# Two VectorE operations of a weight conversion moved between the row maxima of lone attention

## The chip, the cores and the metric

The kernel runs on one core of a Trainium2 chip. The metric is the device time of one execution in microseconds (us).

## The reference, cut to what matters

Sliding-window attention (2 batches, 8 heads, 768 positions, 64 wide; 8 global keys and the last 96) feeds two expert layers.

```python
scores = scale * np.matmul(q, k.transpose(0, 1, 3, 2)) + bias      # bias: -slope * distance
scores = np.where(keep, scores, -1e9)
a = np.exp(scores - np.max(scores, axis=-1, keepdims=True))
a = a / (np.sum(a, axis=-1, keepdims=True) + 1e-09)
attn = np.matmul(a, v)                                             # (1536, 512) after merging heads
h = attn @ w_in1;  x = (np.maximum(h, 0) + alpha * np.minimum(h, 0)) @ w_out1
h = x @ w_in2;     y = (P(h) / (Q(h) + 1e-6)) @ w_out2             # cubic over quadratic in |h|
```

Inputs and outputs are float32, and the weights arrive as 64-bit numbers (two 32-bit words each).

## The kernel before, in words

Attention is cut into 12 blocks of 128 queries, and each block into two half blocks of four heads. A half block is a *slot* u; its two steps z = 2u and 2u + 1 take two heads each. Slots 0 to 9 are lone attention (`alone`, from the start to about 41 us): nothing but attention runs on TensorE. From slot 10 on the joint slots follow (`joint_slot`): the first expert layer's matmuls on L859 and L930 run between the attention of the later slots. Then the layers run by themselves (`plain_slot`).

Every engine executes its instructions in the order in which the code issues them, so the order of the lines in `alone` is the order on each engine. In slot u this is:

- TensorE: scores of slot u (L518), values of slot u - 3 (L595, L597), transposes of the probabilities of slot u - 2 (L574, L576), transposes of the next keys or queries (L460).
- VectorE: in `biased` the scores plus the mask, with the row maximum of each head as a second result (L537: one instruction for a head, and a short one that reads the accumulator; four heads in a slot, on two banks for each step); the reciprocals of the row sums of slot u - 1 (L562, L563); in even slots from 4 on a copy of eight keys (L473) out of the bank in which TensorE's next transposes land; low halves of the output (L608); in odd slots a copy of transposed probabilities (L582).
- ScalarE: exponentials (L544, which need the row maxima), copies out of PSUM, and the first operation of a conversion (L336).
- GpSimd: four normalisations of the probabilities of slot u - 1 (L556, which need the reciprocals), in slot 3 a copy of keys (L501), in slot 4 the sign constants (L223 to L225), and the high part of a conversion (L343).

Between these stands the *conversion* of the weights: 128 x 512 weights arrive as two words each in `stage`, are put together to float32 and split into a high and a low part. It has six operations: ScalarE scales the upper word (L336, into `de`); VectorE shifts it (L337), adds the sign (L338) and adds the bits of the lower word (L340, into `dx`); GpSimd rounds to the high part (L343); VectorE subtracts that from the whole (L346, the low part `winlo` or `woutlo`), and both parts are queued to be spilled to memory. `begin` puts these as a list into `creeps`, and `creep` issues the next entry. `alone` calls `creep` three times a slot, and an entry that does nothing is a pause. A conversion begins at the end of slots 1, 3, 5, 7 and 9. Before the change L336 stands at the end of the odd slot, L337, L338 and L340 in the even slot, L343 in the next odd slot, and L346 is put into the even slot after that, directly ahead of the next conversion's L337. So the conversion's last VectorE operation ends behind the even slot's reciprocals, and L340 is the last VectorE operation ahead of an odd slot's row maxima. In the first joint slot (s == 0, u = 10) the remaining entries are issued at three places. SyncE issues all large transfers, in order.

Of the kernel before, what the change touches and what calls it, by code (L numbers as in the profile page):

```python
# [14 lines left out]
ALU = mybir.AluOpType  # L15
# [42 lines left out]
def flat(t):  # L58
    return t.rearrange("p c f -> p (c f)")


def words(t):
    return flat(t).bitcast(F32)


class Kernel:
# [249 lines left out]
    def begin(self, start):  # L316
        nc = self.nc
        if not start:
            return
        n = self.started  # L320
        self.started += 1
        m, fc, kind, slot = self.plan[n]
        low, e, y = self.staged(n)[:, :, :, 0], self.de[n % 2].bitcast(I32), self.dx[n % 3]
        hi, lo = (flat(self.slots[slot][kind, part]) for part in PARTS)
        x = words(y)

        def kept():
            if m == 0 and fc < KEPT:
                for part, of in zip(PARTS, (hi, lo)):
                    self.unspilled.append((words(self.spilled[fc][kind, part]), of.bitcast(F32)))  # L330
            self.spill()

        last = self.creeps.pop() if self.creeps else lambda: None
        self.creeps.clear()
        self.creeps += [
            lambda: nc.scalar.mul(self.de[n % 2], self.staged(n)[:, :, :, 1].bitcast(F32), 2.0**-112),  # L336
            lambda: (last(), nc.vector.tensor_scalar(y, e, 3, None, ALU.logical_shift_left)),  # L337
            lambda: nc.vector.scalar_tensor_tensor(y, e, -(2**31), y, ALU.bitwise_and, ALU.bitwise_or),  # L338
            lambda: (
                nc.vector.scalar_tensor_tensor(y, low, 29, y, ALU.logical_shift_right, ALU.bitwise_or),  # L340
                self.load_more() if n >= NST else None,
            ),
            lambda: nc.gpsimd.tensor_scalar(hi, x, 1.0, 1.0, ALU.mult, ALU.mult),  # L343
            lambda: None,
            lambda: None,
            lambda: (nc.vector.tensor_sub(lo, x, hi.bitcast(F32)), kept()),  # L346
        ]
# [67 lines left out]
    def attention_window(self, pool, moe):  # L415
        nc, ident, banks = self.nc, self.ident, self.banks
# [39 lines left out]
        def transpose_in(nm, i, bank, cs=slice(0, NC)):  # L456
            src = self.boot[nm, i] if i < 2 else raw[nm][i % 2]
            t = banks[bank].rearrange("p (c t) -> p c t", c=NC)
            for c in range(cs.start, cs.stop):
                nc.tensor.transpose(t[:, c], src[:, 2 * c : 2 * c + 2].rearrange("p h d -> p (h d)"), ident)  # L460
# [42 lines left out]
        def width(z):  # L503
            return P if (z // 4) % NB == 0 else WIN


        def steps_of(u):
            return (2 * u, 2 * u + 1) if 0 <= u < NU else ()

        def scores(u):  # L510
            for z in steps_of(u):
                i, c = divmod(z, 4)
                qb, w = i % NB, width(z)
                w0 = LEAD + i % KEEP * KST - (w - P)
                passes = ((qall, kall),) if i < WHOLE else ((qhi, khi), (qhi, klo), (qlo, khi))
                for e, (q, k) in enumerate(passes):
                    for j, rows in enumerate(HALF):
                        nc.tensor.matmul(  # L518
                            room(z, j),
                            q[i % 2][rows, c],  # L520
                            k[rows, c, w0 : w0 + w],
                            start=e == 0,
                            stop=e == len(passes) - 1,
                        )

        def room(z, j):
            if z < JOIN:
                return banks[4 * (z % 2) + j][:, : width(z)]
            return banks[j][:, 256 * (z % 2) : 256 * (z % 2) + width(z)]

        def biased(u):
            for z in steps_of(u):
                c, w = z % 4, width(z)
                bm = bm0 if w == P else bm1
                for j in range(2):
                    top = stat[u % 3][:, 2 * (z % 2) + j : 2 * (z % 2) + j + 1]
                    nc.vector.tensor_tensor_reduce(  # L537
                        prob[z % 6][:, j, :w], room(z, j), bm[:, 2 * c + j, :], 1.0, 3.0e38, ALU.add, ALU.min, top
                    )
# [18 lines left out]
        def both_ready(u):  # L558
            if steps_of(u):
                r = rec[u % 2]  # L560
                add = nc.vector.tensor_scalar if u < JOIN // 2 else nc.gpsimd.tensor_scalar
                add(r, stat[u % 3][:, 4:8], 1e-9, 1.0, ALU.add, ALU.mult)  # L562
                nc.vector.reciprocal(r, r)  # L563
                for z in steps_of(u):
                    normalise(z)
# [51 lines left out]
        def inputs(u):  # L617
            some = []
            i, odd = divmod(u + 3, 2)
            if not odd and 2 <= i < NBLK:  # L620
                some.append(("k", i, slice(0, NC)))
            i, odd = divmod(u + 2, 2)
            if not odd and 2 <= i < NBLK:
                some.append(("q", i, slice(0, NC)))
            return some
# [12 lines left out]
        def keys_of_all(u):  # L638
            if u % (2 * NB) == 0 and u < NU:
                global_keys(u)  # L640
            if u in (3, 15):
                lead_keys(u)
# [17 lines left out]
        def low_halves():  # L660
            while lows:
                lows.pop(0)()
# [9 lines left out]
        def alone(u):  # L672
            t = 2 * u - JOIN
            if u:
                scores(u)
            if u == 1:
                transpose_in("q", 1, 2)
                self.turn_alpha()
            if u == 2:
                transpose_in(*inputs(1)[0][:2], 3)  # L680
            biased(u)
            if u == 0:
                split_in("q", 0, 7, far, vector=True)
                split_in("k", 1, 3, vector=True)()
            if u == 1:
                split_in("q", 1, 2, vector=True)
            both_ready(u - 1)
            low_halves()
            keys_of_all(u)
            if u < 2:  # L690
                later_masks(range(4 * u, 4 * u + 4))
            values(u - 3)
            if u in WL:
                self.load_next()
            fetches(u)
            if u == 4:
                self.signs()
            exponentials(2 * u)
            if u == 2:
                split_in(*inputs(1)[0][:2], 3)()  # L700
            low = store_x(u - 3)
            self.creep()
            exponentials(2 * u + 1)
            if u == 1:
                self.alpha_ready()
            low()
            self.creep()
            transpose_p(u - 2, 6)
            copy_p(u - 2, 6, both=u % 2 == 1)
            if u > 1:  # L710
                turn_inputs(u)
            self.begin(t in self.starts or t + 1 in self.starts)
            self.creep()
            self.used += u in (2, 4, 6, 8)
# [37 lines left out]
        for u in range(JOIN // 2):  # L752
            alone(u)
# [91 lines left out]
    def moe(self):  # L845
        nc, steps, banks = self.nc, self.steps, self.banks
# [127 lines left out]
        def joint_slot(s, halves):  # L974
            u = JOIN // 2 + s
            opening, turning = halves or (lambda u: None, lambda u: ())
            if s >= CH + 2 and s < CH + 2 + NEARLY:
                self.reload(s - CH - 2)
            opening(u)
            held = []  # L980
            if s == 0:
                self.creep()
            else:
                while self.creeps:
                    self.creep()
                self.tick(True, 2 * s - 1 in self.starts, spread=True, held=held)
                self.join_step(2)
            first(s)
            halves = leaky(s)
            self.join_step(2)  # L990
            if s == 0:
                self.creep()
            lows = turning(u)
            low = halves()
            for high in held:
                high()
            for more in lows:
                more()
            low()
            if s == 0:  # L1000
                self.creep()
            self.tick(True, 2 * s in self.starts, spread=True)
            if s:
                second(s - 1)
            if s == LATE - 1:
                self.tick(True, 2 * s + 1 in self.starts)
                self.spill()
# [125 lines left out]
```

## Time and profile before

| | us |
|---|---|
| median of 3 runs | 620.1 (620.06 to 620.34) |
| the profiled execution | 619.93 |
| its span, first to last instruction | 617.9 |
| TensorE busy in the span | 605.5 |
| VectorE busy in the span | 498.7 |
| ScalarE busy in the span | 404.7 |
| GpSimd busy in the span | 130.5 |

Times in the rows below are microseconds from the start of the span. The engines are PE (TensorE's matmuls), DVE (VectorE), ACT (ScalarE), POOL (GpSimd) and SP (SyncE). L537 is a line of the kernel before. Records of neighbouring instructions of one engine can overlap a little, since the next one starts while the last results are still being written.

### The profile page before, as it was taken

To read this page: it belongs to the slowest core of one execution; us is meant where nothing else is said; L and a number is where in the kernel's file an instruction comes from. 1 tells how busy PE (TensorE), PEld (TensorE's weight loads), DVE (VectorE), ACT (ScalarE), POOL (GpSimd) and SP (SyncE) were. 2 spreads that over 40 slices of the span, in tenths; PEclk is the share of its full clock that TensorE was granted. 3 is DMA by queue.
4 is the path that set the end of the run, shared out by engine and by line. 5 is a ranking of instruction groups with operands and counts; after the bars stand their busy time and mean duration, and the time that the engine had idled before them with its cause. 6 is when DMAs were issued, how large, how long until landed. Compare 5 with 4: busy or idle time off the path is not lost.

```text
span 617.9 us, 9436 instructions
## 1 busy us (share of the span) xinstructions
PE 605.5 (98%) x3187; PEld 497.6 (81%) x3187; DVE 498.7 (81%) x961; ACT 404.7 (66%) x826; POOL 130.5 (21%) x202
## 2 busy tenths in 40 slices
PE   7999999999999999999999999999999999999996
PEld 6678878888888888888888888888888888888884
DVE  6988899776457768668479889999899977788976
ACT  6997777877354444354354587787877766765772
POOL 6863223322100000000000012122222222222221
PEclk9999999999999999999999999999999999999998
DMA  9999999988789433215322401211200000400402
GB/s 217 238 255 282 312 270 316 290 265 268 249 283 350 163 102 118 88 35 158 115 68 75 130 1 34 94 43 39 100 3 32 0 1 0 137 1 1 136 1 74
DMA packets 81570, 82.53 MB, mean 134 GB/s; under 512 B 42010, under 2 KB 58666, under 8 KB 81514
## 3 DMA queue, kind: packets, MB, share of 16 engines
q1 hardware_dynamic: 81334, 81.71, 44.0%
q8 instruction: 27, 0.44, 0.3%
q14 instruction: 29, 0.24, 0.1%
q10 hardware_dynamic: 180, 0.14, 0.1%
HBM read 59.94 MB, written 19.92 MB: 129 GB/s over the span
## 4 chain that ended last, share of the span: by engine, by line
PE 90%; DVE 4%; ACT 2%; issue 1%; DMA 1%; SPq 1%; POOL 0%; ACTq 0%; DVEq 0%
PE bank L859 41%; PE bank L930 41%; PE bank L518 2%; PE bank L595 2%; PE bank L574 1%; PE bank L597 1%; ACT prob L544 1%; PE bank L576 1%; PE bank L460 1%; DMA stage<-in_moe_w_in_dram 1%; DVE prob L537 1%; SPq L230 1%; DVE dx L388 1%; ACT pt L582 0%; DVE dx L387 0%
## 5 line engine op out<-in xcount | busy, mean ns | idle before, releaser
L915 POOL TENSOR_TENSOR glo<-act,ghi 128x512 fp32r<-128x512 f32 (+1 forms) x49 | 62.4, 1274 | 382.7 <-ACT ghi L911 362.6
L859 PE MATMUL bank<-xhi,winhi_f 128*128 128x512 f32 x256 | 68.4, 389 | 0.0
L859 PE MATMUL bank<-xhi,winlo_f 128*128 128x512 f32 x256 | 68.4, 389 | 0.0
L859 PE MATMUL bank<-xlo,winhi_f 128*128 128x512 f32 x256 | 68.4, 389 | 0.0
L556 POOL TENSOR_SCALAR prob<-prob,rec 128x232 f32<-128x232 f32 (+1 forms) x96 | 48.6, 524 | 69.9 <-DVE rec L563 43.8
L867 DVE SCALAR_TENSOR_TENSOR bank<-bank,sg,act 128x512 f32<-128x512 f32 x48 | 36.3, 757 | 31.2 <-ACT act L866 31.1
L870 ACT ACTIVATE ghi<-bank,sg 128x512 fp32r<-128x512 f32 x48 | 33.3, 695 | 39.2 <-DVE bank L867 25.0
L866 ACT ACTIVATE act<-bank,sa 128x512 f32<-128x512 f32 x48 | 32.8, 683 | 37.5 <-PE bank L859 37.3
L859 PEld LDWEIGHTS bank<-xhi,winlo_f 128*128 128x128 f32 x256 | 48.1, 188 | 10.0
L859 PEld LDWEIGHTS bank<-xlo,winhi_f 128*128 128x128 f32 x256 | 48.0, 188 | 10.0
L859 PEld LDWEIGHTS bank<-xhi,winhi_f 128*128 128x128 f32 x256 | 48.0, 188 | 10.0
L544 ACT ACTIVATE prob<-prob,stat 128x232 f32<-128x232 f32 (+1 forms) x96 | 44.7, 469 | 14.6 <-DVE stat L537 12.6
L871 DVE SCALAR_TENSOR_TENSOR glo<-bank,sg,ghi 128x512 fp32r<-128x512 f32 x48 | 35.9, 747 | 18.8 <-PE bank L930 14.3
L882 ACT ACTIVATE stage<-bank 128x512 f32<-128x512 f32 (+1 forms) x49 | 28.8, 588 | 33.0 <-PE bank L859 33.0
L891 DVE SCALAR_TENSOR_TENSOR stage<-stage,abs_b 128x512 f32<-128x512 f32 (+1 forms) x49 | 36.0, 737 | 15.2 <-ACT stage L883 15.1
L397 ACT ACTIVATE de<-stage 128x512 f32<-128x512 f32 x59 | 39.5, 675 | 7.1 <-issue 3.2
L387 DVE SCALAR_TENSOR_TENSOR dx<-de,dx 128x512 int32<-128x512 int32 x59 | 41.1, 697 | 2.0
L388 DVE SCALAR_TENSOR_TENSOR dx<-stage,dx 128x512 int32<-128x512 int32 x59 | 40.9, 693 | 1.6
L911 ACT CAST ghi<-act 128x512 fp32r<-128x512 f32 (+1 forms) x49 | 30.2, 616 | 17.6 <-DVE act L908 15.2
L930 PE MATMUL bank<-wouthi_f,glo 128*128 128x512 f32 x144 | 41.1, 391 | 0.0
L930 PE MATMUL bank<-wouthi_f,ghi 128*128 128x512 f32 x144 | 40.9, 389 | 0.0
L930 PE MATMUL bank<-woutlo_f,ghi 128*128 128x512 f32 x144 | 40.9, 389 | 0.0
(241 smaller groups left out, 1415.7 us busy)
## 6 DMA issues: line engine op xcount, KB each, us to landing
stage<-in_moe_w_in_dram SPq DMA_DIRECT2D x32, 512.0 KB
stage<-in_moe_w_out_dram SPq DMA_DIRECT2D x32, 512.0 KB
part<-saved_f SPq DMA_DIRECT2D x16, 256.0 KB
saved_f<-part SPq DMA_DIRECT2D x12, 256.0 KB
out_dram<-part SPq DMA_DIRECT2D x11, 256.0 KB
rawk<-in_k_dram SPq DMA_DIRECT2D x10, 256.0 KB
rawq<-in_q_dram SPq DMA_DIRECT2D x10, 256.0 KB
va<-in_v_dram SPq DMA_DIRECT2D x10, 240.0 KB
```

What stands on the lines that cost most here:

```text
L387: lambda: nc.vector.scalar_tensor_tensor(y, e, -(2**31), y, ALU.bitwise_and, ALU.bitwise_or),
L388: lambda: nc.vector.scalar_tensor_tensor(y, low, 29, y, ALU.logical_shift_right, ALU.bitwise_or),
L397: nc.scalar.mul(self.de[n % 2], self.staged(n)[:, :, :, 1].bitcast(F32), 2.0**-112)
L544: nc.scalar.activation(p[:, j - e, :w], p[:, j - e, :w], AF.Exp, bias=st[:, j : j + 1], scale=-1.0, accum_out=st[:, 4 + j : 5 + j],)
L556: nc.gpsimd.tensor_scalar(p[:, j, :w], p[:, j, :w], r[:, e + j : e + j + 1], 1.0, ALU.mult, ALU.mult)
L859: nc.tensor.matmul(bk, w["in", a][:, c, :], x[:, c, :], start=e == 0, stop=e == len(seq) - 1)
L867: nc.vector.scalar_tensor_tensor(h, h, sg, t, ALU.mult, ALU.max)
L870: nc.scalar.activation(hi, h, AF.Copy, scale=sg)
L871: return lambda: nc.vector.scalar_tensor_tensor(lo, h, sg, hi.bitcast(F32), ALU.mult, ALU.subtract)
L891: nc.vector.scalar_tensor_tensor(w, w, self.ab[:, 0:1], ab, ALU.add, ALU.mult)
L915: nc.gpsimd.tensor_tensor(lo, u, hi.bitcast(F32), ALU.subtract)
L930: nc.tensor.matmul(y[d], lhs, rhs, start=begin and e == 0, stop=last and e == 2)
```

## The change

The list of a conversion gets its entries in other places, and `biased` calls a function between its two steps, that is, between the row maxima of the first two heads and of the last two. Lone attention passes `creep`, so there is a fourth entry a slot, the first of the slot. The low part L346 of the conversion before becomes an entry of its own, first in the list after L336, and falls between the maxima of an even slot. L340 falls between the maxima of the next odd slot, after a pause at the even slot's end. GpSimd's L343 and the other operations keep their place. In the first joint slot one more entry is issued at the first place.

```diff
@@ begin @@
         self.creeps += [
             lambda: nc.scalar.mul(self.de[n % 2], self.staged(n)[:, :, :, 1].bitcast(F32), 2.0**-112),
-            lambda: (last(), nc.vector.tensor_scalar(y, e, 3, None, ALU.logical_shift_left)),
+            last,
+            lambda: nc.vector.tensor_scalar(y, e, 3, None, ALU.logical_shift_left),
             lambda: nc.vector.scalar_tensor_tensor(y, e, -(2**31), y, ALU.bitwise_and, ALU.bitwise_or),
+            lambda: None,
             lambda: (
                 nc.vector.scalar_tensor_tensor(y, low, 29, y, ALU.logical_shift_right, ALU.bitwise_or),
                 self.load_more() if n >= NST else None,
             ),
             lambda: nc.gpsimd.tensor_scalar(hi, x, 1.0, 1.0, ALU.mult, ALU.mult),
             lambda: None,
-            lambda: None,
             lambda: (nc.vector.tensor_sub(lo, x, hi.bitcast(F32)), kept()),
         ]
@@ attention_window @@
-        def biased(u):
+        def biased(u, between=lambda: None):
             for z in steps_of(u):
+                if z % 2:
+                    between()
                 c, w = z % 4, width(z)
@@ alone @@
-            biased(u)
+            biased(u, self.creep)
@@ joint_slot @@
             if s == 0:
                 self.creep()
+                self.creep()
```

The first place is VectorE in slot 4, from the second head's row maximum on. `prob` with `stat` is a row maximum of one head (a line `ISA stat` reads its accumulator), `rec` are the reciprocals, `kall` is the key copy, `winlo` the low part of the conversion before and `dx` the next conversion. Before:

```order
L537 ISA prob_276,stat_281<-bank_84,bm_309 128x232
L537 ISA stat_281 128x1
L537 ISA prob_277,stat_281<-bank_87,bm_309 128x232
L537 ISA stat_281 128x1
L537 ISA prob_277,stat_281<-bank_88,bm_309 128x232
L537 ISA stat_281 128x1
L562 TENSOR_SCALAR rec_284<-stat_280 128x4
L563 RECIPROCAL rec_284<-rec_284 128x4
L473 COPY kall<-bank_86 128x4x8
L346 TENSOR_TENSOR winlo__113<-dx_97,winhi__112 128x512
L337 TENSOR_SCALAR dx_98<-de_96 128x512
```

And in the changed kernel (its lines are numbered up to four higher):

```order
L540 ISA prob_276,stat_281<-bank_84,bm_309 128x232
L540 ISA stat_281 128x1
L347 TENSOR_TENSOR winlo__113<-dx_97,winhi__112 128x512
L540 ISA prob_277,stat_281<-bank_87,bm_309 128x232
L540 ISA stat_281 128x1
L540 ISA prob_277,stat_281<-bank_88,bm_309 128x232
L540 ISA stat_281 128x1
L565 TENSOR_SCALAR rec_284<-stat_280 128x4
L566 RECIPROCAL rec_284<-rec_284 128x4
L474 COPY kall<-bank_86 128x4x8
L338 TENSOR_SCALAR dx_98<-de_96 128x512
```

The low part has moved ahead of the last two row maxima, the reciprocals and the key copy; slots 6 and 8 read alike.

The second place is VectorE at the border of slots 2 and 3, where the first conversion ends its first three operations. Before:

```order
L338 SCALAR_TENSOR_TENSOR dx_97<-de_95,dx_97 128x512
L340 SCALAR_TENSOR_TENSOR dx_97<-stage_91,dx_97 128x512
L537 ISA prob_274,stat_280<-bank_83,bm_309 128x232
L537 ISA stat_280 128x1
L537 ISA prob_274,stat_280<-bank_84,bm_309 128x232
L537 ISA stat_280 128x1
L537 ISA prob_275,stat_280<-bank_87,bm_309 128x232
```

And in the changed kernel:

```order
L339 SCALAR_TENSOR_TENSOR dx_97<-de_95,dx_97 128x512
L540 ISA prob_274,stat_280<-bank_83,bm_309 128x232
L540 ISA stat_280 128x1
L540 ISA prob_274,stat_280<-bank_84,bm_309 128x232
L540 ISA stat_280 128x1
L342 SCALAR_TENSOR_TENSOR dx_97<-stage_91,dx_97 128x512
L540 ISA prob_275,stat_280<-bank_87,bm_309 128x232
```

The third operation has moved behind the first two row maxima; slots 5, 7 and 9 read alike.

The third place is SyncE's queue around slot 6: `dwinhi` and `dwinlo` are spills of a conversion's two parts, `stage` the next weights and `rawk` a block of keys. Before:

```order
L301 DMA stage_91<-in_moe_w_out_dram 128x1024
L230 DMA rawk_254<-in_k_dram 128x8x64
L244 DMA dwinhi_f<-winhi__116 128x512
L244 DMA dwinlo_f<-winlo__117 128x512
L301 DMA stage_92<-in_moe_w_in_dram 128x4x256
```

And in the changed kernel:

```order
L244 DMA dwinhi_f<-winhi__116 128x512
L244 DMA dwinlo_f<-winlo__117 128x512
L301 DMA stage_91<-in_moe_w_out_dram 128x1024
L230 DMA rawk_254<-in_k_dram 128x8x64
L301 DMA stage_92<-in_moe_w_in_dram 128x4x256
```

The two spills have moved ahead of the weights and the keys.

## Rows read from the trace of the kernel before

**Rows 1.** The page's busy time: us, share of the span, instructions.

```profile
PE 605.5 (98%) x3187; PEld 497.6 (81%) x3187; DVE 498.7 (81%) x961; ACT 404.7 (66%) x826; POOL 130.5 (21%) x202
```

**Rows 2.** Stretches: busy us per engine (instructions), granted clock, DMA share, GB/s.

```profile
core 0: us, PE busy (x) PEld busy (x) DVE busy (x) ACT busy (x) POOL busy (x), PEclk, DMA share, GB/s
25.80:29.40 3.60, 3.02 (x36) 2.34 (x31) 3.53 (x14) 3.60 (x13) 3.17 (x5) 1.00 1.05 307
```

**Rows 3.** Chain of waits, 0 to 70 us: start, length, what.

```profile
16.85 1.76 POOL prob L556 x4
...
19.68 0.94 DVE winlo__113 L346
...
41.90 2.78 PE bank L859 x12
...
61.46 2.76 PE bank L930 x12
...
68.09 0.68 DVE winlo__113 L377
```

**Rows 4.** Waits of PE, 60 to 100 us: total, times, longest.

```profile
PE bank L859 <- DVE glo L871: 1.0, 1, 1.0
```

**Rows 5.** Timeline of ACT: start, length, instruction [idle before <-releaser].

```profile
15.46 0.49 ACT L544 ACTIVATE prob<-prob,stat 128x232 f32<-128x232 f32 x1 [0.68 <-DVE stat L537]
...
23.02 0.49 ACT L544 ACTIVATE prob<-prob,stat 128x232 f32<-128x232 f32 x1 [0.46 <-DVE stat L537]
```

**Rows 6.** Timeline of POOL, slots 3 to 7.

```profile
19.02 0.62 POOL L343 TENSOR_SCALAR winhi__112<-dx 128x512 fp32r<-128x512 f32 x1
19.62 3.38 POOL L556 TENSOR_SCALAR prob<-prob,rec 128x232 f32<-128x232 f32 x4
...
23.70 0.22 POOL L225 TENSOR_TENSOR sa<-sg,al 128x16 f32<-128x16 f32 x1
...
26.18 0.62 POOL L343 TENSOR_SCALAR winhi__116<-dx 128x512 fp32r<-128x512 f32 x1
...
31.55 1.76 POOL L556 TENSOR_SCALAR prob<-prob,rec 128x232 f32<-128x232 f32 x4 [1.00 <-ACT xhi L607]
33.28 0.61 POOL L343 TENSOR_SCALAR winhi__120<-dx 128x512 fp32r<-128x512 f32 x1
```

**Rows 7.** Timeline of DVE, slots 4 to 10.

```profile
18.24 0.40 DVE L537 CUSTOM_DVE_ANT_0 prob<-bank,bm 128x232 f32<-128x232 f32 x1
...
19.68 0.94 DVE L346 TENSOR_TENSOR winlo__113<-dx,winhi__112 128x512 fp32r<-128x512 f32 x1 [0.30 <-POOL winhi__112 L343]
...
25.89 0.40 DVE L537 CUSTOM_DVE_ANT_0 prob<-bank,bm 128x232 f32<-128x232 f32 x1
...
27.02 0.68 DVE L346 TENSOR_TENSOR winlo__117<-dx,winhi__116 128x512 fp32r<-128x512 f32 x1
...
29.05 0.75 DVE L340 SCALAR_TENSOR_TENSOR dx<-stage,dx 128x512 int32<-128x512 int32 x1
...
31.18 0.18 DVE L563 RECIPROCAL rec<-rec 128x4 f32<-128x4 f32 x1
...
33.23 0.39 DVE L537 CUSTOM_DVE_ANT_0 prob<-bank,bm 128x232 f32<-128x232 f32 x1
...
34.24 0.68 DVE L346 TENSOR_TENSOR winlo__121<-dx,winhi__120 128x512 fp32r<-128x512 f32 x1
...
48.15 0.68 DVE L340 SCALAR_TENSOR_TENSOR dx<-stage,dx 128x512 int32<-128x512 int32 x1
```

**Rows 8.** Timeline of PE, slots 8 and 9.

```profile
34.59 0.60 PE L460 MATMUL bank<-part,rawq 128*128 128x128 f32 x4
...
36.54 0.44 PE L595 MATMUL bank<-pt,va 128*64 128x128 f32 x4 [0.36 <-ACT pt L582]
...
38.41 0.60 PE L460 MATMUL bank<-part,rawk 128*128 128x128 f32 x4
```

**Rows 9.** Waits of all engines, 9 to 60 us.

```profile
ACT de L336 <- DMA stage<-in_moe_w_in_dram: 0.4, 1, 0.4
```

## The prediction

> **What bounds the kernel now.** I read the page's busy shares first, then the stretches, then the chain of waits, then the timelines of single engines. TensorE is busy 98% of the span and VectorE 81% [rows 1], so a change can only show where TensorE waits. The changed slots lie in the lone attention, some 12 to 42 us. There the stretch from 25.8 to 29.4 has VectorE at 3.53 and ScalarE at 3.60 of 3.60 us, TensorE at 3.02, all at granted clock 1.00 [rows 2]: the small matmuls wait for the others. The chain of waits shows how: in slot 4 it runs on GpSimd through the four normalisations of L556 and then into VectorE's L346 at 19.68; from 41.90 it is the first joint matmuls on L859 [rows 3]. What decides is how late those start. Behind them little is free: TensorE's longest wait from 60 to 100 us is one of 1.0 us for VectorE [rows 4], where the chain itself runs through VectorE (L377 at 68.09) [rows 3]. A delay at 42 us should therefore arrive at the end nearly whole.
>
> **The change part by part.** Nothing is removed or added in work: the same instructions stand in another order on VectorE, and three pairs of spills and one load on SyncE's queue. I call the third operation of a conversion L340 and the subtraction of its low part L346, by their lines before.
>
> *L340 from ahead of an odd slot's four row maxima to their middle.* The first two maxima come 0.67 us earlier (one L340), the last two end as before. ScalarE waited 0.68 us at 15.46 and 0.46 us at 23.02 for exactly these maxima [rows 5]; both waits can go. That is worth 1.14 us to ScalarE, but only if nothing later holds it.
>
> *L346 from behind an even slot's reciprocals to the middle of its row maxima.* It reads the high part that GpSimd makes at L343, and L343 stands on GpSimd behind the four normalisations of the slot before, which wait for that slot's reciprocal. The change leaves these where they were. In the trace L343 ends at 19.64 (19.02 + 0.62), 26.80 and 33.89 [rows 6]. The third maximum of slots 4, 6 and 8, in front of which L346 now stands, started at 18.24, 25.89 and 33.23 [rows 7]. Each time L346 would come too early, by 1.40, 0.91 and 0.66 us, and 0.04 us for the hand-over (19.64 to 19.68). Before, it waited once, for 0.30 us [rows 7]. Behind the waiting L346 stand the last two maxima, the reciprocals, the copy of eight keys and the next conversion; ScalarE waits for the maxima, GpSimd for the reciprocals, TensorE for the copy (its next transposes go into the bank that the copy reads).
>
> Adding the waits up gives 1.44 + 0.95 + 0.70 - 0.30 = 2.8 us, but each delays what the next one is measured against, so I go round the loop instead, from one L346 to the next. From L346 to the place of L340: 27.02 to 29.05, 2.03 us. From there through the maxima to the end of the reciprocal: 29.05 to 31.36 (31.18 + 0.18), 2.31. From there through four normalisations and L343: to 33.89, 2.53. Hand-over 0.04. New in the loop are the last two maxima, the reciprocals and the key copy, which now follow L346: 25.89 to 27.02 is 1.13 and 33.23 to 34.24 is 1.01, mean 1.07 [rows 6, 7]. The loop is 7.98 us; before, L346 came after 7.34 (19.68 to 27.02) and 7.22 us (27.02 to 34.24) [rows 7].
>
> The first L346 stays at 19.68, since slot 3 has the same work in another order. Those of slots 6 and 8 come at 27.66 and 35.64, the latter 1.40 late. Behind it: L346 itself, 0.68 long at 27.02 (0.94 at 19.68 beside GpSimd's normalisations, which can't have begun now) [rows 7], then 1.01, so the key copy is done at 37.3. TensorE's transposes at L460 started at 34.59 without a wait for it [rows 8]; now they start at about 37.3, 2.7 later. TensorE then waited 0.36 us for ScalarE at 36.54 [rows 8]; ScalarE is less late than that, so this wait is swallowed. The joint matmuls of 41.90 come 2.3 us late. The records of neighbouring VectorE instructions overlap by some hundredths, which the loop counts twice over; I take 2.2.
>
> *GpSimd beside VectorE.* The four normalisations of an even slot took 3.38 us (19.62), those of an odd slot 1.76 (31.55) [rows 6]; the first lay beside L346 and the rest of the conversion, the second beside operations that read PSUM. After the change L346 is past and L340 is gone to the next slot, so two of four such operations are left and I take half of the 1.6 us. This matters in slot 4: normalisations and sign constants took 19.62 to 23.92 (23.70 + 0.22), 4.30 us [rows 6], and start now at some 21.5, behind L346, two maxima and the reciprocals. With half of the excess they end at 25.0, just when slot 5's reciprocal is there (19.68 + 1.07 + 2.03 + 2.31 = 25.1); with all of it at 25.8, so that the loop is once 0.7 longer, and slot 8's transposes wait some tenths for the same reason: 3.0 to 3.3 us in all. The lower end is the loop with every overlap taken off: 1.7. The Trainium skill (SBUF — State Buffer, Who interferes with whom) says that a VectorE instruction with two SBUF inputs and a GpSimd one that reads SBUF exclude each other. The rows agree (3.38 beside 1.76 us), and by that rule the excess goes with the operations, as taken; by unchanged rows the sum would be 3.2.
>
> *The first joint slot.* L340 of the fifth conversion (48.15) [rows 7] moves behind a reciprocal, the slot's maxima and a low half, and the high part with it. Those weights are first used by the L930 matmuls at 61.46 [rows 3]; even 4 us later is early enough, so 0, and without that cover what it is later.
>
> *SyncE.* In slots 4, 6 and 8 two spills of 256 KB move ahead of a raw block's load; the tightest is the one that TensorE turns at 38.41 [rows 8]. From 9 to 60 us the only wait for a transfer is 0.4 us at the first weights [rows 9], and all consumers come later now, so 0.
>
> **Sum.** The profiled execution took 619.93 us with a span of 617.9, the median of the three runs 620.1. 619.93 + 2.2 = 622.1; on the median, 622.3.
>
> **Rivals.** *The early maxima win.* If L343 were ready when L346 comes, only the gain of the odd slots is left: 1.14 us at ScalarE, which is full from 25.8 to 29.4 [rows 2], so 619.0. For it: both waits are real. Against: the three times at which L343 ended; it would have to be earlier by up to 1.4 us, and what stands ahead of it on GpSimd is released by reciprocals that don't move forward. *The delay is given back.* The joint stage starts 2.2 us late, but its transfers are then ahead, and TensorE's wait of 1.0 us there [rows 4] could vanish: 1.2 us remain, 621.3. Against: that wait is for VectorE, whose work there is itself started by TensorE. *TensorE's clock falls.* In slot 4 the key copy would come at 21.4 (19.68 + 0.68 + 1.07), and TensorE, which went on without such a pause before, would stand still for up to 2 us. If its granted clock fell from 1.00 (2.4 GHz) to 1.2 GHz for one slot, its 3.0 to 3.6 us of work per 3.6 [rows 2] would double: 3.3 more, 625.6. The Trainium skill (TensorE: Matmul & The Clock Gate, Part 1: The HAM clock gate) has the array fall to the lower clock after idling; no run here shows it for such waits.
>
> **How the numbers follow.** Forecast 0.74; early maxima 0.09; given back 0.11; clock 0.06. Within 0.2% (1.24 us, about what a measurement of this kernel can tell from no change) lies 618.9 to 621.3. Slower: 0.70 of the forecast and the clock's 0.06, 0.76. Same: 0.04 of the forecast, 0.11, and 0.05 of the early maxima, 0.20. Faster: 0.04. The forecast's own bounds are 621.8 and 623.4; the range goes down to 620.7 to take in the given-back case with room, and up to 623.5.
>
> **What would show it.** Right: on VectorE a wait for GpSimd's high part in front of L346 in slots 4, 6 and 8, of 1.4, about 1 and about 1 us, the last two maxima behind it, ScalarE waiting for them there; L346 some 7.9 us apart; normalisations of even slots near 2.5 us; the first joint matmul at 43.9 to 44.2 instead of 41.7, and the same distance at the end. Wrong: no wait in front of L346, or a first joint matmul before 42.5; or it starts late and the distance has gone by 100 us; or a granted clock under 1.00 in the lone slots.

## The result, and the profile after

The changed kernel took 623.4 us (median of 6 runs, 622.79 to 624.39), the kernel before 620.13 us in the same comparison (6 runs, 620.06 to 620.37). The ratio is 1.0054, 95% interval 1.0044 to 1.0064: slower by 3.3 us. The forecast was 622.3, the range 620.7 to 623.5. The profiled execution took 623.42 us with a span of 621.5.

The page's busy times, which answer to [rows 1], hardly differ:

```profile
PE 607.0 (98%) x3187; PEld 499.3 (80%) x3187; DVE 497.6 (80%) x961; ACT 406.0 (65%) x826; POOL 130.0 (21%) x202
```

TensorE's busy time grew by 1.5 us; that is not more work but a slower clock, as the stretches show below. (L347 is now the low part, L342 the third operation, L345 the high part, L559 the normalisations, L461 the input transposes, L519 the scores, L862 the first joint matmuls.) VectorE's timeline has the low parts of slots 4, 6 and 8, which answer to [rows 7]; the columns are start, length, instruction, and the idle time before it with its releaser:

```profile
20.33 0.69 DVE L347 TENSOR_TENSOR winlo__113<-dx,winhi__112 128x512 fp32r<-128x512 f32 x1 [1.73 <-POOL winhi__112 L345]
...
28.38 0.40 DVE L540 CUSTOM_DVE_ANT_0 prob<-bank,bm 128x232 f32<-128x232 f32 x1 [0.71 <-PE bank L519]
...
29.16 0.69 DVE L347 TENSOR_TENSOR winlo__117<-dx,winhi__116 128x512 fp32r<-128x512 f32 x1
...
37.04 0.69 DVE L347 TENSOR_TENSOR winlo__121<-dx,winhi__120 128x512 fp32r<-128x512 f32 x1 [0.67 <-POOL winhi__120 L345]
```

In slots 4 and 8 VectorE stands still for GpSimd's high part. In slot 6 it stands still earlier, 0.71 us for TensorE's scores in front of the slot's first maximum, and the high part is then just ready when the low part's turn comes. From one low part to the next it is 8.83 and 7.88 us; before it was 7.34 and 7.22. TensorE's timeline answers to [rows 8]:

```profile
22.09 1.11 PE L461 MATMUL bank<-part,rawq 128*128 128x128 f32 x4 [2.35 <-DVE kall L474]
23.12 1.92 PE L519 MATMUL bank<-kall,qall 64*128 64x232 f32 x8
...
38.80 0.66 PE L461 MATMUL bank<-part,rawq 128*128 128x128 f32 x4 [0.99 <-DVE kall L474]
...
45.46 1.17 PE L862 MATMUL bank<-xhi,winhi__112 128*128 128x512 f32 x4
```

Before, the transposes of slot 8 came at 34.59 with no wait [rows 8]. Now TensorE waits for VectorE's key copy, 2.35 us in slot 4 and 0.99 in slot 8, and the first joint matmul comes at 45.46. Note also the lengths at 22 to 25 us: four transposes take 1.11 us there and 0.66 at 38.80; the scores' eight records take 1.92, and 1.05 in slot 4 of the kernel before. The stretches say why (busy us per engine, granted clock, DMA share, GB/s):

```profile
19.74:22.09 2.35, 0.00 (x1) 0.01 (x1) 1.73 (x9) 0.90 (x4) 0.56 (x1) 1.00 0.99 275
22.10:25.50 3.40, 3.40 (x18) 2.41 (x20) 2.40 (x8) 2.83 (x10) 3.18 (x7) 0.50 1.15 222
25.60:29.20 3.60, 3.60 (x46) 3.01 (x44) 2.67 (x14) 3.10 (x11) 2.47 (x6) 1.00 0.92 264
```

TensorE did nothing from 19.74 to 22.09, and then its granted clock was 0.50 (1.2 GHz) up to 25.5 us and 1.00 (2.4 GHz) again after it. VectorE's first maximum of slot 5 had to wait for those slow scores:

```profile
24.30 0.40 DVE L540 CUSTOM_DVE_ANT_0 prob<-bank,bm 128x232 f32<-128x232 f32 x1 [1.00 <-PE bank L519]
```

The chain of waits, which answers to [rows 3], shows the new loop: a slot's normalisations on GpSimd, the high part there, the low part on VectorE, the transposes on TensorE, and round again until the joint slots begin.

```profile
17.49 1.77 POOL prob L559 x4
19.26 0.45 POOL kall L502
19.71 0.60 POOL winhi__112 L345
20.33 0.69 DVE winlo__113 L347
22.09 1.11 PE bank L461 x4
23.19 1.85 PE bank L519 x8
...
45.68 2.79 PE bank L862 x12
...
71.88 0.68 DVE winlo__113 L378
```

Nothing is given back later: the low part of L378 is at 71.88 where it was at 68.09 [rows 3], 3.8 late, and of TensorE's waits from 64 to 104 us the longest is still the one for VectorE of [rows 4]:

```profile
PE bank L862 <- DVE glo L874: 1.1, 1, 1.1
```

### The profile page after: what moved, and what is told of

Same layout as the page of the kernel before. It is cut to its first block, busy times and chain, and to the rows that moved or that the text cites. A ratio compares the mean times of both kernels' runs of the same rounds, so it can differ in the third digit from the quotient of the medians.

```text
span 621.5 us, 9433 instructions
## 1 busy us (share of the span) xinstructions
PE 607.0 (98%) x3187; PEld 499.3 (80%) x3187; DVE 497.6 (80%) x961; ACT 406.0 (65%) x826; POOL 130.0 (21%) x202
## 3 DMA queue, kind: packets, MB, share of 16 engines
q1 hardware_dynamic: 81334, 81.71, 43.9%
## 4 chain that ended last, share of the span: by engine, by line
PE 90%; DVE 4%; DMA 2%; POOL 1%; issue 1%; ACT 1%; SPq 1%; POOLq 0%; ACTq 0%
PE bank L862 41%; PE bank L933 41%; PE bank L519 2%; PE bank L598 2%; DMA stage<-in_moe_w_in_dram 2%; PE bank L577 1%; PE bank L461 1%; PE bank L600 1%; PE bank L579 1%; POOL prob L559 1%; DVE prob L540 1%; SPq L230 1%; DVE dx L389 1%; DVE dx L388 0%; DVE dx L387 0%
## 5 line engine op out<-in xcount | busy, mean ns | idle before, releaser
L862 PE MATMUL bank<-xhi,winhi_f 128*128 128x512 f32 x256 | 68.4, 389 | 0.0
L862 PE MATMUL bank<-xhi,winlo_f 128*128 128x512 f32 x256 | 68.4, 389 | 0.0
L862 PE MATMUL bank<-xlo,winhi_f 128*128 128x512 f32 x256 | 68.4, 389 | 0.0
L559 POOL TENSOR_SCALAR prob<-prob,rec 128x232 f32<-128x232 f32 (+1 forms) x96 | 47.5, 513 | 74.4 <-DVE rec L566 43.3
L873 ACT ACTIVATE ghi<-bank,sg 128x512 fp32r<-128x512 f32 x48 | 33.3, 695 | 39.5 <-DVE bank L870 25.5
L862 PEld LDWEIGHTS bank<-xhi,winhi_f 128*128 128x128 f32 x256 | 48.1, 188 | 10.0
L862 PEld LDWEIGHTS bank<-xlo,winhi_f 128*128 128x128 f32 x256 | 48.1, 188 | 10.0
L862 PEld LDWEIGHTS bank<-xhi,winlo_f 128*128 128x128 f32 x256 | 48.0, 188 | 9.9
```

Of the source, the lines that this page charges most:

```text
L559: nc.gpsimd.tensor_scalar(p[:, j, :w], p[:, j, :w], r[:, e + j : e + j + 1], 1.0, ALU.mult, ALU.mult)
L862: nc.tensor.matmul(bk, w["in", a][:, c, :], x[:, c, :], start=e == 0, stop=e == len(seq) - 1)
L873: nc.scalar.activation(hi, h, AF.Copy, scale=sg)
```

## The experiments

Two theories stood at the start. *Waits alone*: the low part waits for the high part in every even slot, and that is all. *Waits and clock*: the waits cost about 2.4 us, and the pause that they make in slot 4 lowers TensorE's clock, which costs 0.9 more. Beside them stood the prediction's rivals on the early maxima and its zero for SyncE. In the diffs, the list is that of one conversion's steps in their order.

**Third operation alone.**

```diff
-            last,
-            lambda: nc.vector.tensor_scalar(y, e, 3, None, ALU.logical_shift_left),
+            lambda: None,
+            lambda: (last(), nc.vector.tensor_scalar(y, e, 3, None, ALU.logical_shift_left)),
```

> Only the third operation stands between an odd slot's row maxima; the low part is back behind the even slot's reciprocals. Theory (the low part waits there for GpSimd's high part, and TensorE's clock falls in the pause): no such wait, granted clock 1.00, ScalarE's two waits of 0.68 and 0.46 us gone, 0.5 to 1.0 us faster than before, some 619.3. Rival 1 (it is the interruption of the row maxima in the odd slots that costs): most of the 3.3 us is still there, some 622 to 623. Rival 2 (the moved spills on the transfer queue cost): the spills are back in their old places in slots 4, 6 and 8, so the time is as before, 620.1.

Measured: 619.87 us, ratio to before 0.9995 (0.9986 to 1.0004): no difference. Its first weights landed late, at 11.48 instead of 10.75, and yet the first joint matmul is at 42.05 instead of 41.68; the low parts have no wait and stand 7.01 and 6.89 us apart:

```profile
21.03 0.68 DVE L347 TENSOR_TENSOR winlo__113<-dx,winhi__112 128x512 fp32r<-128x512 f32 x1
...
28.04 0.68 DVE L347 TENSOR_TENSOR winlo__117<-dx,winhi__116 128x512 fp32r<-128x512 f32 x1
...
34.93 0.68 DVE L347 TENSOR_TENSOR winlo__121<-dx,winhi__120 128x512 fp32r<-128x512 f32 x1
```

So the early maxima do shorten the loop, by 0.33 us each time (7.34 and 7.22 before), but of the 1.14 us that ScalarE waited the time shows no more than a few tenths. The 0.5 to 1.0 us that the theory gave were missed. This half of the change isn't what makes it slower; the time is also what the rival on the spills gave, and the runs on the spills below decide about that one.

**Low part alone.**

```diff
-            lambda: None,
             lambda: (
                 nc.vector.scalar_tensor_tensor(y, low, 29, y, ALU.logical_shift_right, ALU.bitwise_or),
                 self.load_more() if n >= NST else None,
             ),
+            lambda: None,
             lambda: nc.gpsimd.tensor_scalar(hi, x, 1.0, 1.0, ALU.mult, ALU.mult),
```

> Only the low part stands between an even slot's row maxima; the third operation is back ahead of the odd slot's maxima. Theory: the wait for the high part is there in slots 4, 6 and 8 with 1.4 to 1.7, about 1 and about 1 us, and the clock falls in slot 4: 2.5 to 3.5 us slower than before, 622.6 to 623.6, and no faster than the whole change. Rival 1 (the odd slots cost): near 620.1 to 620.6.

Measured: 622.76 us, ratio 1.0048 (1.0034 to 1.0061). The three waits are there. The fall of the clock, which was expected too, is not in this profile: the granted clock stayed at 1.00 in slots 4 and 5, after a pause of TensorE of 2.01 us:

```profile
20.11 0.69 DVE L347 TENSOR_TENSOR winlo__113<-dx,winhi__112 128x512 fp32r<-128x512 f32 x1 [1.49 <-POOL winhi__112 L345]
...
28.11 0.69 DVE L347 TENSOR_TENSOR winlo__117<-dx,winhi__116 128x512 fp32r<-128x512 f32 x1 [0.79 <-POOL winhi__116 L345]
...
36.09 0.69 DVE L347 TENSOR_TENSOR winlo__121<-dx,winhi__120 128x512 fp32r<-128x512 f32 x1 [0.77 <-POOL winhi__120 L345]
```

The low part's move makes the kernel slower by itself; without a fall of the clock it steps at 8.00 and 7.98 us, the 7.98 of the prediction's loop.

**The high part ahead of the normalisations.** If the low part waits because GpSimd's high part stands behind the odd slot's normalisations, it should not wait once that part is issued ahead of them.

```diff
                 nc.vector.scalar_tensor_tensor(y, low, 29, y, ALU.logical_shift_right, ALU.bitwise_or),
+                nc.gpsimd.tensor_scalar(hi, x, 1.0, 1.0, ALU.mult, ALU.mult),
...
-            lambda: nc.gpsimd.tensor_scalar(hi, x, 1.0, 1.0, ALU.mult, ALU.mult),
+            lambda: None,
```

> The whole change, but GpSimd's high part is issued right behind the third operation, ahead of the odd slot's four normalisations instead of behind them. Theory: the low part finds it ready, its waits in slots 4, 6 and 8 go to 0, TensorE does not pause, clock 1.00; what is left is the gain at ScalarE: 0.5 to 1.2 us faster than before, 619.0 to 619.6. Rival 1 (the interruption of row maxima itself costs): still 622 to 623. Rival 2 (the normalisations become late instead, by one high part of 0.62 us in each of three odd slots): 621 to 622.

Measured: 620.92 us, ratio 1.0019 (1.0007 to 1.0032): most of the loss is gone (0.7 us are left by the medians, 620.92 - 620.23 in this comparison, 1.2 by the ratio), and so are the waits in front of the low part. The gain of 0.5 to 1.2 us that was expected did not come. The twelve runs lie far apart, from 619.89 to 623.62, and the three slowest of them (623.06 and above) have the lowest mean clocks, 0.994 to 0.995. What is left in the profiled execution, which took 621.84 us, is a wait that no theory had, in TensorE's timeline of slot 9:

```profile
39.90 0.63 PE L462 MATMUL bank<-part,rawk 128*128 128x128 f32 x4 [1.40 <-DMA rawk<-in_k_dram]
...
43.20 1.17 PE L863 MATMUL bank<-xhi,winhi__112 128*128 128x512 f32 x4
```

This is the raw block of keys that the change puts behind two spills of 256 KB.

**The same with the spills in their old place on SyncE.** The low part's step only notes its spill; it is queued at the next step, behind the fetches.

```diff
-            last,
-            lambda: nc.vector.tensor_scalar(y, e, 3, None, ALU.logical_shift_left),
+            lambda: (setattr(self, "hold", True), last(), setattr(self, "hold", False)),
+            lambda: (self.spill(), nc.vector.tensor_scalar(y, e, 3, None, ALU.logical_shift_left)),
...
-            self.spill()
+            if not self.hold:
+                self.spill()
```

> The kernel of e3_high_early (the whole change, GpSimd's high part right behind the third operation, ahead of the odd slot's normalisations), and the spills of a conversion queued on SyncE where the kernel before has them, behind the fetches of the even slot. Theory (the spills moved ahead cost something as soon as the waits for the high part no longer cover them): TensorE's wait of 1.40 us for the raw keys in slot 9 of e3_high_early goes, the first joint matmul comes at about 41.8 instead of 43.20, the median is 1.2 us below e3_high_early's, about 619.7, no slower than the kernel before. Rival (the keys are late because all transfers are, wherever the spills stand): the wait stays above 1 us and the median at 620.9.

Measured: 619.88 us, ratio to before 0.9998 (0.9989 to 1.0007). The wait is gone and the first joint matmul comes at 41.41:

```profile
38.14 0.60 PE L464 MATMUL bank<-part,rawk 128*128 128x128 f32 x4
...
41.41 1.17 PE L865 MATMUL bank<-xhi,winhi__112 128*128 128x512 f32 x4
```

So the moved spills cost this version about 1 us: 620.92 beside 619.88, and 0.9 when each is taken against the kernel before of its own comparison. All eleven runs lie between 619.13 and 620.84, so the slowest runs of the version before this one are gone as well; how much of the 1 us is the wait and how much their lower clock was not separated. The rival that late normalisations cost 1 to 2 us is out as well, since the high part stands ahead of them here too. With both obstacles away, the whole change is worth nothing measurable.

**The whole change with the spills in their old place** (the same edit, the high part left where the change has it).

> The whole change, but the spills queued on SyncE where the kernel before has them. Theory (in the changed kernel the waits for the high part cover the spills' move, as the prediction said): the waits in front of the low part stay at 0.7 to 1.7 us, the first joint matmul at 45 to 45.5, the median within 0.6 us of the changed kernel's 623.4. Rival (the moved spills are part of the 3.3 us, by the keys' lateness or by contention): the median falls by 1 us or more, to 622.4 or below.

Measured: 623.43 us, ratio 1.0057 (1.0044 to 1.0071), as the change itself. The waits are 1.41, 0.74 and 0.71 us, the low parts 7.95 and 7.93 apart. The first joint matmul came at 44.51, ahead of the expected 45 to 45.5, and the clock stayed at 1.00 in the lone slots of this profile:

```profile
20.21 0.69 DVE L349 TENSOR_TENSOR winlo__113<-dx,winhi__112 128x512 fp32r<-128x512 f32 x1 [1.41 <-POOL winhi__112 L347]
```

```profile
44.51 1.17 PE L864 MATMUL bank<-xhi,winhi__112 128*128 128x512 f32 x4
```

In the changed kernel the waits of VectorE do hide the spills' move.

**TensorE kept busy in slot 4.** Eight extra matmuls of a constant, then four, ahead of the turn of the inputs; nothing reads their result. (Each stands as two records in the trace.)

```diff
+            if u == 4:
+                for _ in range(8):
+                    nc.tensor.matmul(banks[1][:, 256:384], ident, ident, start=True, stop=True)
             if u > 1:
                 turn_inputs(u)
```

> The whole change, and in slot 4 eight extra matmuls of 128x128 into an unused part of a bank, ahead of the transposes that wait for the key copy, so that TensorE works in most of the pause of 2.35 us. Theory (waits of the low part some 2.3 us, the fall of the clock some 1 us): granted clock 1.00 up to the tail, L461 of slot 4 at 0.6 instead of 1.11 us, 0.7 to 1.2 us faster than the change, 622.2 to 622.7. Rival (the clock costs nothing because others are late anyway): 623.4 as the change.

Measured with eight: 622.69 us, ratio 1.0039 (1.0026 to 1.0052), and clock 1.00 from 19 to 41 us in the profile. This profiled execution, 623.31 us and the slowest of its five, had a clock of 0.50 earlier, from 16 to 18 us, and its low part of slot 4 waited only 0.39 us, so it says little about slot 4. And the extra matmuls ran from 21.03 to 23.0, beyond the time at which the key copy was done (22.05 + 0.16), and so took back part of what the clock gave:

```profile
21.03 1.97 PE L715 MATMUL bank<-part 128*128 128x128 f32 x16
22.84 0.60 PE L461 MATMUL bank<-part,rawq 128*128 128x128 f32 x4
```

> The whole change, with four extra 128x128 matmuls of a constant on TensorE in slot 4 ahead of the turn of the inputs (half of e4_busy, which ran on into the transposes' own time), into a bank's unused part; nothing reads them. They end near 20.8, and TensorE then stands still for about 1.3 us instead of 2.35. Theory (the fall of the granted clock to 0.50 from 22.1 to 25.5 us costs about 0.9 us): the clock stays at 1.00 from 22 to 26, the first step from low part to low part falls from 8.83 to about 7.9, and the median to about 622.5. Rival (the fall costs nothing that the waits would not take anyway): the clock may stay up, but the step stays above 8.6 and the median at 623.4.

Measured with four: 622.53 us, ratio 1.0036 (1.0022 to 1.0050). TensorE's timeline, VectorE's low parts with the first maximum of slot 5 between them, and the stretch that answers to the slow one above:

```profile
19.66 1.07 PE L715 MATMUL bank<-part 128*128 128x128 f32 x8
22.17 0.66 PE L461 MATMUL bank<-part,rawq 128*128 128x128 f32 x4 [1.44 <-DVE kall L474]
22.76 1.05 PE L519 MATMUL bank<-kall,qall 64*128 64x232 f32 x8
...
44.70 1.17 PE L865 MATMUL bank<-xhi,winhi__112 128*128 128x512 f32 x4
```

```profile
20.41 0.69 DVE L347 TENSOR_TENSOR winlo__113<-dx,winhi__112 128x512 fp32r<-128x512 f32 x1 [1.72 <-POOL winhi__112 L345]
...
23.45 0.40 DVE L540 CUSTOM_DVE_ANT_0 prob<-bank,bm 128x232 f32<-128x232 f32 x1
...
28.36 0.69 DVE L347 TENSOR_TENSOR winlo__117<-dx,winhi__116 128x512 fp32r<-128x512 f32 x1 [0.73 <-POOL winhi__116 L345]
```

```profile
22.10:25.50 3.40, 3.33 (x36) 2.74 (x37) 3.32 (x14) 3.40 (x13) 3.19 (x6) 1.00 1.20 252
```

The wait in slot 4 is the same 1.72 us, the transposes begin at the same time (22.17 beside 22.09), but the clock is 1.00, the first maximum of slot 5 comes at 23.45 instead of 24.30, and the step from low part to low part is 7.95 instead of 8.83. The median is 0.9 us below that of the changed kernel (623.4; 623.43 with the old spills, in the same comparison as this one), as the theory of waits and clock said. The mean granted clock of the single runs agrees: 0.992 to 0.997 in the six of the changed kernel, 0.997 to 0.999 in the five of this one.

**Third operation moved, high part ahead of the normalisations, low part in its old place.** This is the version to which the others point: the shorter loop, and no wait.

> Of the change only the third operation's move to the middle of an odd slot's maxima, and GpSimd's high part right behind it, ahead of the odd slot's normalisations; the low part and the spills stand where the kernel before has them. Theory (the early maxima's gain shows only where nothing behind waits for GpSimd): no wait in front of the low part, ScalarE's waits in the odd slots gone, the first joint matmul at about 41.2 plus what the start is late, the median 0.3 to 0.8 us below the kernel before: 619.3 to 619.8. Rival (the high part ahead of the normalisations delays them by its 0.62 us in each odd slot, and their transposes with them): 620.5 to 621.

Measured: 619.64 us, ratio to before 0.9990 (0.9981 to 0.9999), 0.45 us below the kernel before by the medians: the fastest of all, by less than the 0.2% that a measurement can tell from no change. The first joint matmul is at 41.02, with no wait in front of the low parts. The profiled execution itself took 621.97 us, as TensorE's clock was 0.50 from 66.8 to 70.2 us in it, after pauses in the second joint slot: TensorE was busy 4.78 of the 6 us from 60 to 66.

```profile
60.00:66.00 6.00, 4.78 (x32) 3.65 (x30) 2.97 (x5) 3.25 (x7) 0.00 (x0) 1.00 1.04 338
66.80:70.20 3.40, 3.40 (x27) 2.95 (x24) 2.02 (x11) 2.81 (x11) 1.42 (x4) 0.50 0.99 340
```

## Why the prediction was right, and where it was not

The direction, the place and the mechanism were right; the time came out 1.1 us above the forecast, 0.9 by TensorE's clock and 0.2 by the waits. That it still lies in the range is luck in part: the forecast's own upper bound of 623.4 was there for the case that GpSimd's whole excess of 1.6 us stays in slot 4. Only 0.58 us of it stayed, and no wait came of it; the clock, which the sum had at nothing, took up that room.

Two of the prediction's own signs went against it. A granted clock under 1.00 in the lone slots was named as a sign of being wrong, and it is there. The first joint matmul, foreseen at 43.9 to 44.2, came at 45.46; where the clock stayed up in the lone slots from slot 4 on and nothing else was changed in the loop, it came at 44.51, 44.51 and 44.70 (low part alone, old spills, four extra matmuls), 2.83, 2.83 and 3.02 us late. Of this 0.43, 0.53 and 0.73 are a later first low part (20.11, 20.21 and 20.41 beside 19.68), so that the loop gave 2.3 to 2.4.

*The loop of waits* was sized well. The prediction went round it with 7.98 us; where the clock stayed up it measured 8.00 and 7.98 (low part alone), 7.95 and 7.93 (old spills), 7.95 (four extra matmuls). The waits themselves, foreseen at 1.4, about 1 and about 1 us, were 1.73, hidden and 0.67, and 1.72, 0.73 and 0.71 with the extra matmuls. This term, taken as 2.2 us, is 2.4: 622.53 - 620.09 with four extra matmuls, which leave only the waits. That the change is slower is shown by the run that moves the high part, which takes the waits away and most of the loss with them, and by the one that also has the spills in their old place (0.9998).

*The first low part* was to stay at 19.68; it came at 20.33. The first weights, for which ScalarE's conversion waits, landed 0.40 us later (11.15 beside 10.75), as it differs from run to run (10.96 to 11.51 in the experiments); by VectorE's second operation of slot 2 0.22 us of that were left (13.82 beside 13.60). The other 0.43 us arose in slot 3, which the prediction took as neutral: the first maximum there waited 0.33 us for GpSimd, and the third operation took 0.85 us in the middle of the maxima, 0.11 more than ahead of them.

*TensorE's clock* is the step that failed. The prediction had the pause (the key copy at 21.4, TensorE still for up to 2 us; it was 2.35), but put the fall of the clock at nothing in its sum and kept it as a rival on top of the waits, with a chance of 0.06 and a price of 3.3 us. The fall came, and cost 0.9. The price was too high since it doubled all the work of a slot: the clock was low from 22.1 to 25.5 us, but only the transposes and scores up to the first maximum are on the path, 24.30 - 22.09 = 2.21 us beside 23.45 - 22.17 = 1.28. The 3.3 us are thus 2.4 of waits and 0.9 of clock. The runs of one kernel say the same: of the five with the old spills, the profiled one, whose clock stayed at 1.00 in the lone slots, took 622.59 us at a mean clock of 0.998, the other four 623.42 to 624.69 at 0.991 to 0.997. The Trainium skill (TensorE: Matmul & The Clock Gate, Part 1: The HAM clock gate) has the array fall to the lower clock after idling; the runs agree, since it fell after 2.35 us without a matmul and stayed up when half of that was filled. It also stayed up after pauses of 2.01 and 2.09 us, so a pause of about this length does not bring the fall every time.

*GpSimd beside VectorE* was foreseen at near 2.5 us for the normalisations of an even slot, down from 3.3 to 3.4. They took 2.35, 2.88 and 2.88 us:

```profile
22.15 2.35 POOL L559 TENSOR_SCALAR prob<-prob,rec 128x232 f32<-128x232 f32 x4 [1.85 <-DVE kall L474]
26.76 1.77 POOL L559 TENSOR_SCALAR prob<-prob,rec 128x232 f32<-128x232 f32 x4 [1.05 <-ACT xhi L610]
...
30.97 2.88 POOL L559 TENSOR_SCALAR prob<-prob,rec 128x232 f32<-128x232 f32 x4 [1.85 <-DVE kall L474]
```

The prediction counted half of four operations; better is to count one by one, and without L337, which reads one tile only. VectorE's operations with two inputs in SBUF that begin beside them:

```profile
22.61 0.69 DVE L339 SCALAR_TENSOR_TENSOR dx<-de,dx 128x512 int32<-128x512 int32 x1
...
31.44 0.68 DVE L339 SCALAR_TENSOR_TENSOR dx<-de,dx 128x512 int32<-128x512 int32 x1
...
32.84 0.69 DVE L342 SCALAR_TENSOR_TENSOR dx<-stage,dx 128x512 int32<-128x512 int32 x1
```

That is one in slot 4 and two in slot 6; before, slot 4 had three, the low part [rows 7] and the second and third operations behind it. The excess over 1.77 is 0.58, 1.11 and, before, 1.6 us [rows 6]: about 0.55 each, a little less than such an operation's 0.68. So the rule that the two exclude each other (SBUF — State Buffer, Who interferes with whom, in the Trainium skill) gave nearly the right size once the operations were counted, and half of the excess, the prediction's figure, lies between what slots 4 and 6 show.

*SyncE's reorder at 0* was right for this kernel and for the reason given, as the kernel with the old spills shows (623.43). The reason was the cover, and the prediction did not price its loss: where the waits were taken away, 1.40 us of wait for the keys and about 1 us of time came up.

*The early maxima* can't win, as said, while the low part waits; and with that wait gone they bring a few tenths at most, not 1.14 us: 619.87 alone. Where the rest of their shorter loop goes was not followed. *Given back* is refuted by the L862 wait of 1.1 us, which stayed, and by the 3.8 us at L378. The fifth conversion's later third operation cost nothing: in the kernel with that operation alone it stands as late, and the time is that of before.

## What to carry over

Before an operation is moved forward on one engine, look up when its input is ready on the other; here three end times of GpSimd against three start times on VectorE gave the loss before any run. A pause that the move opens on TensorE has two prices, the wait and, in the executions in which the clock then falls, the slower matmuls behind it; the second counts only the matmuls on the path. And a reorder that is free because something else is late stops being free in the version that mends the lateness: test the two together.

## What the hardware showed that was not expected

The fall of the granted clock is not the same in each execution of similar kernels: after pauses of 2.01 us (low part alone) and 2.09 us (old spills) in slot 4 the profiled executions kept 1.00, after 2.35 us it fell. The two kernels whose first weights came latest (11.48 and 11.51 us) had the fall in slot 3 instead, here the third operation alone:

```profile
15.00:18.00 3.00, 3.00 (x20) 2.10 (x17) 2.72 (x13) 2.56 (x10) 1.08 (x4) 0.50 1.25 234
```

So a loss by clock can stand in one slot in one execution and in another in the next; that the later start is what moves it was not tried.
